# A router's scratch moved from the value products' PSUM bank to banks of its own and to SBUF

## The chip, the cores and the metric

One Trainium2 chip (trn2), one NeuronCore. The metric is the time of one execution on the device in microseconds (us); all times below are in us unless marked otherwise.

## What is computed

Attention over 4 batches, 8 heads, 768 tokens of 64 values, in which a query sees only keys with the same 6-bit hash; then a mixture of experts over the 3072 tokens of 512 values, each going to the one of 8 experts with the largest logit.

```python
q_bucket = sum((q @ proj > 0) * powers); k_bucket = sum((k @ proj > 0) * powers)
scores = where(q_bucket == k_bucket, scale * q @ k.T, -1e9)
x = (softmax(scores) @ v).transpose(0, 2, 1, 3).reshape(B * S, H * D)
logits = x @ w_gate + modality_bias[modality_id]
e_idx = argmax(logits); gate_w = max(softmax(logits))
out[e_idx == e] = gate_w * (relu(x @ w1[e]) @ w2[e])      # for each expert e
```

## The kernel before

`attention()` (L92) runs over 16 pairs of heads, four pairs for a batch. For each pair TensorE computes score tiles, first for the row maxima (`psm`, maxima by VectorE at L241 and L247, two tiles ahead at most) and then for the exponentials (`pss`, L295 and L296, exponentials by ScalarE at L307 and L314 into `pb`); GpSimd adds the `pb` tiles for the row sums (L317, `sp`); TensorE multiplies them with the values (L341, `psu`); ScalarE copies the result to `ut` (L346), which gives the two tiles of `psu` back to the next pair; L359 turns `sp` into sums.

Before a pair's softmax its queries' and keys' hash bits are prepared two pairs ahead (L200, L222). The order of TensorE and of SyncE's queue is written by hand: loop i goes over one pair, and a string of the table PLAN for each of its six rows names what comes next: S two score matmuls' worth, M a maximum, T the preparation, A value products, Q sums, x and y the transposes of `finish_x` (L417, `xs`), G, g, h, k, f, e, w, E one piece of the list of pieces that finishes a batch. VectorE, ScalarE and GpSimd get their order from a scheduler that goes by the order of the program.

When four pairs are done their batch is finished piece by piece: `finish` (L366) sums over the heads into `gl` and the logits (L399 to L403), `route` (L598) takes the maximum (`rm`), the exponent (`rex`), and the one-hot of the chosen expert (`oh`, L612), counts with twelve small matmuls how many tokens chose which expert before each token (L617, L619; the running counts are `run`), forms the gate (L629 to L631) and the token's place in the table (`posi`, L637), and scatters six columns of it with indirect DMAs issued by GpSimd (L642). Batch 0 is finished in the loops of pairs 4 to 7, batch 1 in 8 to 11, batch 2 in 12 to 15, batch 3 in the expert stage. A generator yields once for each piece; in `finish_last` (L426) the first UPTO pieces of batch 2 run, then the early slots (`early_slots`, L708: which blocks of which expert can be gathered before the last batch is routed), then their tables are loaded through SyncE's queue (`early_tables`, L724), then batch 2's scatters.

Router temporaries do not have tiles of their own while attention runs. `Spots` (L80) hands out columns 256 to 512 of `psu1`, the PSUM bank whose first 256 columns are the second part of the value products:

```python
shared = ps_u.tile([P, MAIN], F32, name="psu1")
spot.psum = shared[:, REST:MAIN]
...
t["u"] = [ps_u.tile([P, MAIN], F32, name="psu0"), shared[:, 0:REST]]
```

The waits between engines are kept for a tile, so a row of VectorE in this scratch and a value product of TensorE wait for each other. In the profile both are named `psu`. After attention the scratch is an SBUF tile (`spot.psum = None`, L518).

Of the kernel before, what the change touches and what calls it, by code (L numbers as in the profile page):

```python
# [28 lines left out]
P = 128  # L29
# [4 lines left out]
RELIEF = ()  # L34
UPTO = 12
PLAN = (
# [42 lines left out]

class Spots:  # L80

    psum = None

    def __call__(self, pool, shape, name, at):
        if self.psum is None:
            return pool.tile(shape, F32, name=name)
        n = int(np.prod(shape[1:]))
        ap = self.psum[:, at:at + n]
        return ap if len(shape) == 2 else ap.rearrange("p (a e) -> p a e", a=shape[1])


def attention(ctx, actx, tc, a, x_d, route, setup, early_slots, early_tables, latest, adds, bias, later, spot):  # L92
    nc = tc.nc
# [16 lines left out]
    sm = actx.enter_context(tc.tile_pool(name="sm", bufs=4))  # L110
# [25 lines left out]
    ident = fconst.tile([P, P], F32, name="ident")  # L136
# [192 lines left out]
    def weigh():  # L329

        for i in range(NPR):
            t = st[i]
            t["u"] = [ps_u.tile([P, MAIN], F32, name="psu0"), shared[:, 0:REST]]
            for part in range(2):
                w = COLS[part].stop - COLS[part].start
                nc.tensor.matmul(t["u"][part][:, 0:w], vsb[i % 2], t["lone"][:, COLS[part]], start=True, stop=False, skip_group_check=True)
            for kt in range(NT):
                for part in range(2):
                    w = COLS[part].stop - COLS[part].start
                    for h in range(2):  # L340
                        nc.tensor.matmul(t["u"][part][64 * h:64 * h + 64, 0:w], t["v"][:, h, kt], t["pb"][kt][:, h, COLS[part]], start=False, stop=(kt == NT - 1), skip_group_check=True)  # L341
                if kt == NT - 1:
                    ut = upool.tile([P, S], F32, name="ut")
                    for part in range(2):
                        w = COLS[part].stop - COLS[part].start
                        nc.scalar.copy(out=ut[:, COLS[part]], in_=t["u"][part][:, 0:w])  # L346
                    t["ut"] = ut
                yield
# [17 lines left out]
    def finish(b):  # L366
# [23 lines left out]
        gl = bp.tile([P, NT, 9, 8], F32, name="gl")  # L390
        with tc.issue_after(exps[0]):
            nc.scalar.copy(out=gl[:, :, 8], in_=bias[:, b * NT:(b + 1) * NT])
        for w in range(2):
            n = 4 if w == 0 else 2
# [6 lines left out]
            yield  # L401
        lg = spot(bp, [P, NT, 8], "lg", 0)
        nc.vector.tensor_reduce(out=lg, in_=gl.rearrange("p t h e -> p t e h"), axis=AX.X, op=ALU.add)  # L403
        yield
        yield from route(b, lg, ps_x)

# [42 lines left out]
    with tc.manual_schedule(engines={mybir.EngineType.PE, mybir.EngineType.SP}):  # L449
# [67 lines left out]
        sums(NPR - 1)  # L517
        spot.psum = None  # L518
    return finish, finish_x, ps_x, ident


N = B * S
E = 8
# [6 lines left out]
EARLY = CFG["early"]  # L530
EARLYB = 2
# [17 lines left out]
def router(ctx, tc, a, x_d, tab):  # L549
    nc = tc.nc  # L550
# [44 lines left out]

    scattered, latest, adds, later, counts, spot = [], [], [], [], [], Spots()

    def route(b, lg, ps):  # L598
        l = lg
        m = wk.tile([P, NT], F32, name="rm")  # L600
        nc.vector.tensor_reduce(out=m, in_=l, axis=AX.X, op=ALU.max)
        d = spot(wk, [P, NT, E], "rd", 48)
        nc.vector.tensor_tensor(out=d, in0=l, in1=m.unsqueeze(2).broadcast_to([P, NT, E]), op=ALU.subtract)
        ex = wk.tile([P, NT, E], F32, name="rex")
        nc.scalar.activation(ex, d, AF.Exp)
        yield
        w = spot(wk, [P, NT, E], "rw", 96)
        nc.vector.scalar_tensor_tensor(out=w, in0=d, scalar=0.0, in1=rev.unsqueeze(1).broadcast_to([P, NT, E]), op0=ALU.is_ge, op1=ALU.mult)
# [3 lines left out]
        nc.vector.tensor_tensor(out=oh, in0=w, in1=wm.unsqueeze(2).broadcast_to([P, NT, E]), op=ALU.is_equal)  # L612
        yield
        pp = ps.tile([P, HALF], F32, name="psx")
        for j in range(NT):
            lhs = tri if j == 0 else onesb
            nc.tensor.matmul(pp[:, j * E:NT * E], lhs, oh[:, 0:NT - j].rearrange("p t e -> p (t e)"), start=(j == 0), stop=False, skip_group_check=True)  # L617
        for j in range(NT):
            nc.tensor.matmul(pp[:, 64:64 + E], onesb, oh[:, j], start=False, stop=(j == NT - 1), skip_group_check=True)  # L619
        rk = spot(wk, [P, NT, E], "rk", 144)  # L620
        nc.vector.tensor_tensor(out=rk, in0=pp[:, 0:NT * E].rearrange("p (t e) -> p t e", e=E), in1=run[b % 2].unsqueeze(1).broadcast_to([P, NT, E]), op=ALU.add)
        if b == EARLYB - 1:
            counts.append(spot(wk, [P, E], "counts", 200))
            nc.vector.tensor_tensor(out=counts[0], in0=run[b % 2], in1=pp[:, 64:64 + E], op=ALU.add)
        nc.vector.tensor_tensor(out=run[(b + 1) % 2], in0=run[b % 2], in1=pp[:, 64:64 + E], op=ALU.add)
        yield
        rec = recs[:, b]
        sm = spot(wk, [P, NT], "rsum", 192)
        nc.vector.tensor_reduce(out=sm, in_=ex, axis=AX.X, op=ALU.add)  # L629
        nc.vector.tensor_scalar(out=sm, in0=sm, scalar1=1e-9, scalar2=None, op0=ALU.add)  # L630
        nc.vector.reciprocal(rec[:, :, 1].bitcast(F32), sm)  # L631
        yield
        nc.vector.tensor_tensor(out=rk, in0=rk, in1=oh, op=ALU.mult)
        pos = spot(wk, [P, NT], "pos", 192)
        nc.vector.tensor_reduce(out=pos, in_=rk, axis=AX.X, op=ALU.add)
        posi = wk.tile([P, NT], I32, name="posi", bufs=2)
        nc.vector.tensor_copy(out=posi, in_=pos)  # L637
        yield
# [19 lines left out]
    def above(cnt, row, name):  # L658
        g = spot(wk, [P, E, 12], "sg", 0)
        nc.vector.tensor_tensor(out=g, in0=cnt.unsqueeze(2).broadcast_to([P, E, 12]), in1=step[:, row], op=ALU.is_gt)  # L660
        nb = spot(wk, [P, E], name, 208)
        nc.vector.tensor_reduce(out=nb, in_=g, axis=AX.X, op=ALU.add)
        return nb

    def cumulate(nb, name):
        c2 = spot(wk, [P, E, E], "sc2", 96)
        nc.vector.tensor_tensor(out=c2, in0=low, in1=nb.unsqueeze(1).broadcast_to([P, E, E]), op=ALU.mult)
        cu = spot(wk, [P, E], name, 216)
        nc.vector.tensor_reduce(out=cu, in_=c2, axis=AX.X, op=ALU.add)
        cx = spot(wk, [P, E], name + "x", 224)  # L670
        cs = cu
        if spot.psum is not None:
            cs = wk.tile([P, E], F32, name=name + "s")
            nc.vector.tensor_reduce(out=cs, in_=c2, axis=AX.X, op=ALU.add)
        nc.vector.tensor_tensor(out=cx, in0=cs, in1=nb, op=ALU.subtract)
        return cu, cx

    def assign(n, cu, cx, first, size, out):

        sel = spot(wk, [P, n, E], f"sel{n}", 160)  # L680
        sl = slot[:, 0:n].unsqueeze(2).broadcast_to([P, n, E])
# [4 lines left out]
        nc.vector.tensor_tensor(out=t, in0=sel, in1=eid.unsqueeze(1).broadcast_to([P, n, E]), op=ALU.mult)  # L686
        r = spot(wk, [P, n], f"selr{n}", 192)
        nc.vector.tensor_reduce(out=r, in_=t, axis=AX.X, op=ALU.add)
        nc.vector.tensor_copy(out=out[:, 0], in_=r)
        yield  # L690
        w = spot(wk, [P, E], "selw", 232)
        if size:
# [363 lines left out]
```

## Time and profile before

| | before |
|---|---|
| median of 3 runs | 790.35 us (789.85 to 791.34) |
| the profiled execution, own time | 790.72 us |
| its span | 788.9 us |
| TensorE busy | 747.6 us (95%) |
| VectorE busy | 477.8 us (61%) |
| ScalarE busy | 414.8 us (53%) |
| GpSimd busy | 445.6 us (56%) |

The profile is of one execution. The span goes from the first to the last instruction. An engine's busy time is what its instructions take; time in front of a row in square brackets is idle time of that engine, with the instruction whose end released it. PE is TensorE, DVE VectorE, ACT ScalarE, POOL GpSimd, SP SyncE. A name such as L341 is a line of the kernel.

### The profile page before, as it was taken

Reading aid. Unit: us, or ns where it says so; the run is one execution under the profiler, and the core shown is the slowest. Engines: PE = TensorE matmul, PEld = TensorE weight load, DVE = VectorE, ACT = ScalarE, POOL = GpSimd, SP = SyncE. Lnnn points to the kernel's source line nnn. Section 1 sums busy time; section 2 is a strip of 40 time slices with the busy share of each in tenths; the row PEclk is TensorE's granted clock in tenths of the full one; section 3 lists DMA queues with packets and bytes.
Section 4 is the critical chain, followed back from the end, with each engine's and each line's share of the span. In section 5 each row is a group of like instructions: output and inputs, shape, how many; then the busy total and the mean of one; then the engine's idle time right before and its main releaser. Section 6 shows DMA issues by size and latency. Waiting matters only on the chain.

```text
span 788.9 us, 11622 instructions
## 1 busy us (share of the span) xinstructions
PE 747.6 (95%) x4060; PEld 520.3 (66%) x4060; DVE 477.8 (61%) x829; ACT 414.8 (53%) x732; POOL 445.6 (56%) x325
## 2 busy tenths in 40 slices
PE   5899999999999999999998999999999999999996
PEld 2565566555656566665555546878888888888885
DVE  5777677577777768767766667744344343742422
ACT  3666576666557566666554455333243334643423
POOL 7398988788779888879885982123220204302002
PEclk9999999999999999999999999999999999999999
DMA  6665554264346434454400737376443435844411
GB/s 195 153 189 160 160 130 131 62 160 114 104 126 183 101 97 113 118 170 121 121 22 28 138 77 265 122 126 200 141 139 103 149 105 182 287 117 134 120 55 61
DMA packets 59573, 104.11 MB, mean 132 GB/s; under 512 B 9709, under 2 KB 30957, under 8 KB 59504
## 3 DMA queue, kind: packets, MB, share of 16 engines
q1 hardware_dynamic: 53424, 88.10, 41.0%
q0 software_dynamic: 4928, 13.14, 5.1%
q10 hardware_dynamic: 1152, 2.03, 0.9%
q8 instruction: 34, 0.56, 0.3%
q14 instruction: 35, 0.29, 0.1%
HBM read 59.76 MB, written 13.33 MB: 93 GB/s over the span
## 4 chain that ended last, share of the span: by engine, by line
PE 65%; DVE 11%; issue 10%; ACT 5%; DMA 4%; POOL 3%; SPq 1%; POOLq 0%; ACTq 0%; DVEq 0%
PE psu L341 12%; PE pss L295 8%; PE pss L296 6%; PE hps L846 4%; PE hps L848 4%; PE hps L847 4%; PE yps L892 4%; PE yps L890 4%; PE yps L891 4%; PE psm L239 4%; PE psm L245 2%; ACT pb L307 2%; DVE b_1g L176 2%; PE psx L359 1%; DVE a_0g L266 1%
## 5 line engine op out<-in xcount | busy, mean ns | idle before, releaser
L317 POOL TENSOR_TENSOR sp<-sp,pb 128x768 f32<-128x768 f32 x124 | 233.2, 1908 | 40.5 <-ACT pb L314 37.2
L307 ACT ACTIVATE pb<-pss 128x512 f32<-128x512 f32 x192 | 114.4, 598 | 112.8 <-PE pss L296 96.6
L241 DVE TENSOR_REDUCE mx<-psm 128x1 f32<-128x512 f32 x192 | 130.6, 687 | 55.8 <-PE psm L239 54.8
L341 PE MATMUL psu<-pb,vt 128*64 128x512 f32 (+1 forms) x768 | 136.8, 497 | 4.9 <-DVE eslot L703 2.6
L799 DVE TENSOR_TENSOR w<-raw,w 128x1024 fp32r<-128x1024 f32 x64 | 79.5, 1249 | 94.8 <-ACT w L797 77.2
L797 ACT CAST w<-raw 128x1024 fp32r<-128x1024 f32 x64 | 66.9, 1050 | 73.9 <-PE yps L892 62.7
L341 PEld LDWEIGHTS psu<-pb,vt 128*64 128x64 f32 x768 | 50.9, 138 | 76.2 <-issue 56.4
L817 POOL DMA_INDIRECT xg<-x_d,tb x18 | 22.5, 1248 | 117.8 <-DMA tb<-tab 113.5
L295 PE MATMUL pss<-a_0g 128*128 128x512 f32 x192 | 80.3, 418 | 2.6 <-ACT pb L307 1.7
L890 PE MATMUL yps<-w,hl 128*128 128x512 f32 x208 | 82.7, 398 | 0.0
L892 PE MATMUL yps<-w,hh 128*128 128x512 f32 x208 | 81.3, 391 | 0.0
L891 PE MATMUL yps<-w,hh 128*128 128x512 f32 x208 | 80.9, 389 | 0.0
L846 PE MATMUL hps<-xh,w 128*128 128x512 f32 x192 | 75.6, 394 | 0.8 <-DVE hl L853 0.8
L847 PE MATMUL hps<-xl,w 128*128 128x512 f32 x192 | 74.9, 390 | 0.1
L848 PE MATMUL hps<-xh,w 128*128 128x512 f32 x192 | 74.8, 390 | 0.0
L295 PE MATMUL pss<-a_1g 128*128 128x512 f32 x192 | 67.5, 352 | 4.0 <-ACT pb L314 4.0
L247 DVE TENSOR_REDUCE mx<-psm 128x2 f32<-128x512 f32 x96 | 66.2, 689 | 8.1 <-PE psm L245 4.7
L317 POOL TENSOR_TENSOR sp<-pb,pb 128x768 f32<-128x768 f32 x31 | 56.7, 1850 | 25.2 <-ACT pb L314 25.1
L852 ACT ACTIVATE hh<-hps 128x512 fp32r<-128x512 f32 x48 | 28.6, 598 | 74.5 <-PE hps L848 72.8
L296 PE MATMUL pss<-b_0g 128*128 128x512 f32 x192 | 65.3, 340 | 0.2 <-DMA b_0g<-a_0g 0.2
L296 PE MATMUL pss<-b_1g 128*128 128x512 f32 x192 | 65.0, 339 | 0.0
L853 DVE SCALAR_TENSOR_TENSOR hl<-hps,hh 128x512 fp32r<-128x512 f32 x48 | 33.0, 688 | 52.7 <-ACT hh L852 52.6
(228 smaller groups left out, 1350.2 us busy)
## 6 DMA issues: line engine op xcount, KB each, us to landing
raw<-moe_w SPq DMA_DIRECT2D x64, 512.0 KB
xt<-qk SPq DMA_DIRECT2D x31, 384.0 KB
vt<-v SPq DMA_DIRECT2D x16, 384.0 KB
a_0g<-hx SPq DMA_DIRECT2D x30, 192.0 KB
a_1g<-hx SPq DMA_DIRECT2D x30, 192.0 KB
x_d<-xs SPq DMA_DIRECT2D x18, 256.0 KB
b_1g<-a_1g SPq DMA_DIRECT2D x17, 192.0 KB
b_0g<-a_0g SPq DMA_DIRECT2D x17, 192.0 KB
```

The source lines that it names most:

```text
L241: newest[:] = [nc.vector.tensor_reduce(out=mx[:, qt + j, 1 - h, 0:1], in_=mp, axis=AX.X, op=ALU.max).ins]
L295: nc.tensor.matmul(out, t["s1"][h][:, ks], t["m1"][h][:, cs], start=True, stop=False)
L296: nc.tensor.matmul(out, t["s2"][h][:, ks], t["m2"][h][:, cs], start=False, stop=True)
L307: nc.scalar.activation(t["pb"][kt][:, h, 0:MAIN], sp, AF.Exp, scale=0.125)
L317: add = (nc.vector if h and i in CFG["spd"] else nc.gpsimd).tensor_tensor(out=t["sp"][:, h], in0=(t["pb"][0] if kt == 1 else t["sp"])[:, h ...
L341: nc.tensor.matmul(t["u"][part][64 * h:64 * h + 64, 0:w], t["v"][:, h, kt], t["pb"][kt][:, h, COLS[part]], start=False, stop=(kt == NT - 1 ...
L846: nc.tensor.matmul(hps, lo[:, c, fs], xh[:, c], start=(c == 0), stop=False)
L847: nc.tensor.matmul(hps, hi[:, c, fs], xl[:, c], start=False, stop=False)
L848: nc.tensor.matmul(hps, hi[:, c, fs], xh[:, c], start=False, stop=(c == 3))
L890: nc.tensor.matmul(yps[g], hl[fc][:, gs], hi[:, fb], start=(fc == 0), stop=False)
L891: nc.tensor.matmul(yps[g], hh[fc][:, gs], lo[:, fb], start=False, stop=False)
L892: nc.tensor.matmul(yps[g], hh[fc][:, gs], hi[:, fb], start=False, stop=(fc == 7))
```

## The change

`Spots` is gone. `route` takes `gl`, sums it itself, and is two pieces with PSUM scratch of its own: one tile of the pool `psx` (two banks, also used by transposes, sums and the pattern matmuls) for the logits, their differences and the masked weights, and the rank matmuls' own tile for the ranks, the places and the gate's sum. The value products have `psu0` and `psu1` to themselves. The tables of the early slots (`sg`, `enb`, `sc2`, `ecu`, `ecux`, `sel`, `selr`, `selw`) are SBUF tiles of the pool `wk`. `route` yields twice where it had five yields, and `finish` has one fewer, so UPTO is 8 instead of 12 and every piece behind comes four tokens earlier. The second reduction `ecus`, the copy `counts` and the tile `eleft` are gone.

```diff
-UPTO = 12
+UPTO = 8
...
-    shared = ps_u.tile([P, MAIN], F32, name="psu1")
-    spot.psum = shared[:, REST:MAIN]
...
-            t["u"] = [ps_u.tile([P, MAIN], F32, name="psu0"), shared[:, 0:REST]]
+            t["u"] = [ps_u.tile([P, MAIN], F32, name=f"psu{j}") for j in range(2)]
...
-        lg = spot(bp, [P, NT, 8], "lg", 0)
-        nc.vector.tensor_reduce(out=lg, in_=gl.rearrange("p t h e -> p t e h"), axis=AX.X, op=ALU.add)
-        yield
-        yield from route(b, lg, ps_x)
+        yield from route(b, gl, ps_x)
...
-    def route(b, lg, ps):
-        l = lg
+    def route(b, gl, ps):
+        spot = ps.tile([P, 4, NT, E], F32, name="psx")
+        l, d, w = spot[:, 0], spot[:, 1], spot[:, 2]
+        nc.vector.tensor_reduce(out=l, in_=gl.rearrange("p t h e -> p t e h"), axis=AX.X, op=ALU.add)
         m = wk.tile([P, NT], F32, name="rm")
...
         nc.scalar.activation(ex, d, AF.Exp)
-        yield
-        w = spot(wk, [P, NT, E], "rw", 96)
...
         pp = ps.tile([P, HALF], F32, name="psx")
...
-        rk = spot(wk, [P, NT, E], "rk", 144)
+        rk = pp[:, 128:128 + NT * E].rearrange("p (t e) -> p t e", e=E)
...
-        if b == EARLYB - 1:
-            counts.append(spot(wk, [P, E], "counts", 200))
-            nc.vector.tensor_tensor(out=counts[0], in0=run[b % 2], in1=pp[:, 64:64 + E], op=ALU.add)
         nc.vector.tensor_tensor(out=run[(b + 1) % 2], in0=run[b % 2], in1=pp[:, 64:64 + E], op=ALU.add)
-        yield
...
+        nc.vector.tensor_tensor(out=rk, in0=rk, in1=oh, op=ALU.mult)
+        pos, sm = pp[:, 192:192 + NT], pp[:, 224:224 + NT]
+        nc.vector.tensor_reduce(out=pos, in_=rk, axis=AX.X, op=ALU.add)
+        posi = wk.tile([P, NT], I32, name="posi", bufs=2)
+        nc.vector.tensor_copy(out=posi, in_=pos)
         nc.vector.tensor_reduce(out=sm, in_=ex, axis=AX.X, op=ALU.add)
         nc.vector.tensor_scalar(out=sm, in0=sm, scalar1=1e-9, scalar2=None, op0=ALU.add)
         nc.vector.reciprocal(rec[:, :, 1].bitcast(F32), sm)
-        yield
...
     def above(cnt, row, name):
-        g = spot(wk, [P, E, 12], "sg", 0)
+        g = wk.tile([P, E, 12], F32, name="sg")
...
-        nb = spot(wk, [P, E], name, 208)
+        nb = wk.tile([P, E], F32, name=name)
...
-        if spot.psum is not None:
-            cs = wk.tile([P, E], F32, name=name + "s")
-            nc.vector.tensor_reduce(out=cs, in_=c2, axis=AX.X, op=ALU.add)
-        nc.vector.tensor_tensor(out=cx, in0=cs, in1=nb, op=ALU.subtract)
+        nc.vector.tensor_tensor(out=cx, in0=cu, in1=nb, op=ALU.subtract)
...
-        sel = spot(wk, [P, n, E], f"sel{n}", 160)
+        sel = wk.tile([P, n, E], F32, name=f"sel{n}")
...
-        w = spot(wk, [P, E], "selw", 232)
+        w = wk.tile([P, E], F32, name="selw")
...
-        nb = above(counts[0], 0, "enb")
+        nb = above(run[EARLYB % 2], 0, "enb")
```

The scores' lines L295 and L296 become L281 and L282, the maxima's matmuls L239 and L245 become L225 and L231, L341 becomes L327, L617 and L619 become L599 and L601. Names in the rows that follow: `a_0g` and `b_0g` are operands of the scores, `ident` the transposes' identity, `tri` and `onesb` the rank matmuls' fixed matrices, `klow`, `kslot` and `ke` constants of the tables.

TensorE, first row of the plan in pair 6, where batch 0 is finished. Before:

```order
L245 MATMUL psm<-a_0g_106 128x256 x2
L417 MATMUL psx<-ident,ut 128x128 x4
L295 MATMUL pss<-a_0g_120 128x512
L296 MATMUL pss<-b_0g_122 128x512
L239 MATMUL psm<-a_1g_107 128x512
L295 MATMUL pss<-a_1g_121 128x512
```

With the change:

```order
L231 MATMUL psm<-a_0g_106 128x256 x2
L400 MATMUL psx<-ident,ut 128x128 x4
L599 LDWEIGHTS tri
L599 MATMUL psx<-oh,tri 128x48
L599 LDWEIGHTS onesb
L599 MATMUL psx<-oh,onesb 128x40
```

The twelve rank matmuls (the rows with `oh`, and ten more like them) stand behind the transposes of `xs`; before they stood two plan rows later, behind another group of transposes.

TensorE, second row of the plan in pair 12, where batch 2 is finished. Before:

```order
L296 MATMUL pss<-b_1g_109 128x512
L239 MATMUL psm<-a_1g_114 128x512
L282 MATMUL psx<-va_4113,ones_166 128x128
L295 MATMUL pss<-a_0g_106 128x256
L296 MATMUL pss<-b_0g_108 128x256
L295 MATMUL pss<-a_1g_107 128x256
L296 MATMUL pss<-b_1g_109 128x256
L245 MATMUL psm<-a_1g_114 128x256 x2
```

With the change:

```order
L282 MATMUL pss<-b_1g_109 128x512
L225 MATMUL psm<-a_1g_114 128x512
L268 MATMUL psx<-va_4127,ones_165 128x128
L599 LDWEIGHTS tri
L599 MATMUL psx<-oh,tri 128x48
L599 LDWEIGHTS onesb
```

The rank matmuls stand directly behind the one with `va`; before the value products came first, and the ranks a plan row later.

VectorE in pair 13, the early slots' tables. Before:

```order
L675 TENSOR_TENSOR psu_145<-ecus,psu_145 128x8
L419 TENSOR_TENSOR xs<-psx,rin 128x512
L682 TENSOR_TENSOR psu_145<-psu_145,kslot 128x16
L241 TENSOR_REDUCE mx<-psm 128x1
L684 TENSOR_TENSOR selx_4435<-psu_145,kslot 128x16
L241 TENSOR_REDUCE mx<-psm 128x1
L685 TENSOR_TENSOR psu_145<-psu_145,selx_4435 128x16
L289 TENSOR_TENSOR vs_168<-psx,vs_168 32x64
L686 TENSOR_TENSOR selx_4435<-psu_145,ke_66 128x16
L289 TENSOR_TENSOR vs_168<-psx,vs_168 32x64
L688 TENSOR_REDUCE psu_145<-selx_4435 128x2
L247 TENSOR_REDUCE mx<-psm 128x2
```

With the change:

```order
L646 TENSOR_TENSOR ecux<-ecu,enb 128x8
L233 TENSOR_REDUCE mx<-psm 128x2
L653 TENSOR_TENSOR sel_4360<-ecu,kslot 128x16
L655 TENSOR_TENSOR selx_4362<-ecux,kslot 128x16
L241 TENSOR_REDUCE m_4344<-mx 128x8
L656 TENSOR_TENSOR sel_4360<-sel_4360,selx_4362 128x16
L657 TENSOR_TENSOR selx_4362<-sel_4360,ke_66 128x16
L659 TENSOR_REDUCE selr_4366<-selx_4362 128x2
L660 CAST eslot<-selr_4366 128x2
L227 TENSOR_REDUCE mx<-psm 128x1 x2
L233 TENSOR_REDUCE mx<-psm 128x2
L664 TENSOR_TENSOR selw<-ezero,ecux 128x8
```

The same steps stand earlier among the maxima, and their first operands are no longer in `psu`, so two operands lie in SBUF.

## Rows read from the trace of the kernel before

**Rows 1.** The page, part 1: the span, and each engine's busy time, share and instructions
```profile
span 788.9 us, 11622 instructions
...
PE 747.6 (95%) x4060; PEld 520.3 (66%) x4060; DVE 477.8 (61%) x829; ACT 414.8 (53%) x732; POOL 445.6 (56%) x325
```

**Rows 2.** TensorE's waits: line waited <- for, us in all, times, the longest
```profile
PE psx L264 <- ACT nm L257: 5.2, 4, 1.7
PE pss L295 <- ACT pb L314: 4.0, 11, 0.4
```

**Rows 3.** TensorE's timeline, value products: start us, us, instruction, [idle before <- releaser]
```profile
393.93 1.94 PE L341 MATMUL psu<-pb,vt 128*64 128x256 f32 x12 [1.52 <-ACT rex L605]
...
413.02 1.94 PE L341 MATMUL psu<-pb,vt 128*64 128x256 f32 x12 [0.74 <-DVE psu L662]
...
424.23 3.50 PE L341 MATMUL psu<-pb,vt 128*64 128x256 f32 x12 [2.61 <-DVE eslot L703]
```

**Rows 4.** Windows: stretch, us, then the engines' busy us, granted clock, DMA share, GB/s
```profile
424.00:426.00 2.00, 1.77 (x8) 0.78 (x10) 0.16 (x1) 0.00 (x0) 0.75 (x1) 0.50 0.05 9
```

**Rows 5.** VectorE's timeline, route of batch 0
```profile
190.27 1.02 DVE L403 TENSOR_REDUCE psu<-gl 128x48 f32<-128x432 f32 x1
191.19 1.28 DVE L241 TENSOR_REDUCE mx<-psm 128x1 f32<-128x512 f32 x2
192.47 0.69 DVE L247 TENSOR_REDUCE mx<-psm 128x2 f32<-128x512 f32 x1
193.07 0.68 DVE L419 TENSOR_TENSOR xs<-psx,rin 128x512 f32<-128x512 f32 x1
...
198.53 0.22 DVE L608 SCALAR_TENSOR_TENSOR psu<-psu,ke 128x48 f32<-128x48 f32 x1 [2.12 <-ACT ut L346]
```

**Rows 6.** TensorE's timeline: `xs` transposes, batch 0, and `va` matmuls, batch 2
```profile
192.27 0.60 PE L417 MATMUL psx<-ident,ut 128*128 128x128 f32 x4
...
390.31 0.38 PE L282 MATMUL psx<-va,ones 128*128 128x128 f32 x2
```

**Rows 7.** VectorE's timeline, route of batch 2
```profile
390.48 1.00 DVE L403 TENSOR_REDUCE psu<-gl 128x48 f32<-128x432 f32 x1
391.40 0.67 DVE L241 TENSOR_REDUCE mx<-psm 128x1 f32<-128x512 f32 x1
392.08 0.46 DVE L289 TENSOR_TENSOR vs<-psx,vs 32x64 fp32r<-32x64 f32 x2
...
396.38 0.22 DVE L608 SCALAR_TENSOR_TENSOR psu<-psu,ke 128x48 f32<-128x48 f32 x1 [2.75 <-ACT ut L346]
```

**Rows 8.** TensorE's timeline: waits for `run` and `sp`
```profile
507.67 0.63 PE L417 MATMUL psx<-ident,ut 128*128 128x128 f32 x4 [0.46 <-DVE run L625]
...
452.90 0.84 PE L359 MATMUL psx<-sp,ones 128*32 128x384 f32 x4 [0.67 <-POOL sp L317]
454.65 0.84 PE L359 MATMUL psx<-sp,ones 128*32 128x384 f32 x4 [0.92 <-POOL sp L317]
```

**Rows 9.** VectorE and GpSimd meeting: two-operand rows of both
```profile
242.18 1.04 DVE L176 TENSOR_TENSOR b_1g<-xt,hx 128x768 fp32r<-128x768 f32 x1
...
213.49 2.36 DVE L176 TENSOR_TENSOR b_1g<-xt,hx 128x768 fp32r<-128x768 f32 x1
...
211.41 3.63 POOL L317 TENSOR_TENSOR sp<-sp,pb 128x768 f32<-128x768 f32 x2 [1.78 <-ACT pb L314]
...
450.33 5.10 DVE L317 TENSOR_TENSOR sp<-pb,pb 128x768 f32<-128x768 f32 x1
```

**Rows 10.** VectorE's timeline: a small row of the early tables beside a GpSimd add
```profile
422.57 0.17 DVE L693 TENSOR_TENSOR psu<-ezero,psu 128x8 f32<-128x8 f32 x1
```

**Rows 11.** Windows, line L317 alone: busy us of VectorE and GpSimd, count
```profile
396.00:421.00 25.00, 0.00 (x0) 14.47 (x8) 1.00 0.06 17
```

**Rows 12.** VectorE's timeline: idle ahead of a maximum and of `a_0g`
```profile
410.13 0.69 DVE L241 TENSOR_REDUCE mx<-psm 128x1 f32<-128x512 f32 x1 [0.70 <-PE psm L239]
...
415.30 0.43 DVE L266 SCALAR_TENSOR_TENSOR a_0g<-psx,a_0g 64x256 fp32r<-64x256 f32 x1 [1.02 <-PE psx L264]
```

More of the change, by code (lines that the diff above doesn't have):

```diff
@@ L77, in host_layout, with attention @@
     }
[L80 to L92, printed above, removed]
+def attention(ctx, actx, tc, a, x_d, route, setup, early_slots, early_tables, latest, adds, bias, later):
     nc = tc.nc
@@ L517, in attention @@
         sums(NPR - 1)
-        spot.psum = None
     return finish, finish_x, ps_x, ident
@@ L594, in setup @@
             nc.gpsimd.tensor_copy(out=recs[:, :, :, 0], in_=tok)
-    scattered, latest, adds, later, counts, spot = [], [], [], [], [], Spots()
-    def route(b, lg, ps):
-        l = lg
+    scattered, latest, adds, later = [], [], [], []
+    def route(b, gl, ps):
+        spot = ps.tile([P, 4, NT, E], F32, name="psx")
+        l, d, w = spot[:, 0], spot[:, 1], spot[:, 2]
+        nc.vector.tensor_reduce(out=l, in_=gl.rearrange("p t h e -> p t e h"), axis=AX.X, op=ALU.add)
         m = wk.tile([P, NT], F32, name="rm")
         nc.vector.tensor_reduce(out=m, in_=l, axis=AX.X, op=ALU.max)
-        d = spot(wk, [P, NT, E], "rd", 48)
         nc.vector.tensor_tensor(out=d, in0=l, in1=m.unsqueeze(2).broadcast_to([P, NT, E]), op=ALU.subtract)
@@ L613, in route @@
         yield
+        rec = recs[:, b]
         pp = ps.tile([P, HALF], F32, name="psx")
@@ L619, in route @@
             nc.tensor.matmul(pp[:, 64:64 + E], onesb, oh[:, j], start=False, stop=(j == NT - 1), skip_group_check=True)
-        rk = spot(wk, [P, NT, E], "rk", 144)
+        rk = pp[:, 128:128 + NT * E].rearrange("p (t e) -> p t e", e=E)
         nc.vector.tensor_tensor(out=rk, in0=pp[:, 0:NT * E].rearrange("p (t e) -> p t e", e=E), in1=run[b % 2].unsqueeze(1).broadcast_to([P, NT, E]), op=ALU.add)
-        if b == EARLYB - 1:
-            counts.append(spot(wk, [P, E], "counts", 200))
-            nc.vector.tensor_tensor(out=counts[0], in0=run[b % 2], in1=pp[:, 64:64 + E], op=ALU.add)
         nc.vector.tensor_tensor(out=run[(b + 1) % 2], in0=run[b % 2], in1=pp[:, 64:64 + E], op=ALU.add)
-        yield
-        rec = recs[:, b]
-        sm = spot(wk, [P, NT], "rsum", 192)
+        nc.vector.tensor_tensor(out=rk, in0=rk, in1=oh, op=ALU.mult)
[3 more added lines that the diff above has]
+        nc.vector.tensor_copy(out=posi, in_=pos)
         nc.vector.tensor_reduce(out=sm, in_=ex, axis=AX.X, op=ALU.add)
@@ L631, in route @@
         nc.vector.reciprocal(rec[:, :, 1].bitcast(F32), sm)
-        yield
[L633 to L637, printed above, removed]
         yield
@@ L665, in cumulate @@
     def cumulate(nb, name):
-        c2 = spot(wk, [P, E, E], "sc2", 96)
+        c2 = wk.tile([P, E, E], F32, name="sc2")
         nc.vector.tensor_tensor(out=c2, in0=low, in1=nb.unsqueeze(1).broadcast_to([P, E, E]), op=ALU.mult)
-        cu = spot(wk, [P, E], name, 216)
+        cu = wk.tile([P, E], F32, name=name)
         nc.vector.tensor_reduce(out=cu, in_=c2, axis=AX.X, op=ALU.add)
-        cx = spot(wk, [P, E], name + "x", 224)
-        cs = cu
-        if spot.psum is not None:
-            cs = wk.tile([P, E], F32, name=name + "s")
-            nc.vector.tensor_reduce(out=cs, in_=c2, axis=AX.X, op=ALU.add)
-        nc.vector.tensor_tensor(out=cx, in0=cs, in1=nb, op=ALU.subtract)
+        cx = wk.tile([P, E], F32, name=name + "x")
+        nc.vector.tensor_tensor(out=cx, in0=cu, in1=nb, op=ALU.subtract)
         return cu, cx
     def assign(n, cu, cx, first, size, out):
-        sel = spot(wk, [P, n, E], f"sel{n}", 160)
+        sel = wk.tile([P, n, E], F32, name=f"sel{n}")
         sl = slot[:, 0:n].unsqueeze(2).broadcast_to([P, n, E])
@@ L686, in assign @@
         nc.vector.tensor_tensor(out=t, in0=sel, in1=eid.unsqueeze(1).broadcast_to([P, n, E]), op=ALU.mult)
-        r = spot(wk, [P, n], f"selr{n}", 192)
+        r = wk.tile([P, n], F32, name=f"selr{n}")
         nc.vector.tensor_reduce(out=r, in_=t, axis=AX.X, op=ALU.add)
@@ L715, in early_slots @@
         yield from assign(EARLY, cu, cx, zero, TS, eslot)
-        left = wk.tile([P, E], F32, name="eleft")
-        nc.vector.tensor_scalar(out=left, in0=cx, scalar1=-1.0, scalar2=float(EARLY), op0=ALU.mult, op1=ALU.add)
-        nc.vector.scalar_tensor_tensor(out=early, in0=left, scalar=0.0, in1=nb, op0=ALU.max, op1=ALU.min)
+        nc.vector.tensor_scalar(out=early, in0=cx, scalar1=-1.0, scalar2=float(EARLY), op0=ALU.mult, op1=ALU.add)
+        nc.vector.scalar_tensor_tensor(out=early, in0=early, scalar=0.0, in1=nb, op0=ALU.max, op1=ALU.min)
         yield
@@ L755, in late_slots @@
         return big, sml, tot
-    return route, early_slots, early_tables, (eslot, etb, ete), late_slots, setup, latest, adds, bias, later, spot
+    return route, early_slots, early_tables, (eslot, etb, ete), late_slots, setup, latest, adds, bias, later
 def experts(ctx, tc, a, x_d, tab, out, ps_x, ident, first, adds):
@@ L1012, in body @@
     with ExitStack() as ctx, ExitStack() as actx:
-        route, early_slots, early_tables, early_tiles, late_slots, setup, latest, adds, bias, later, spot = router(ctx, tc, a, x_d, tab)
-        finish, finish_x, ps_x, ident = attention(ctx, actx, tc, a, x_d, route, setup, early_slots, early_tables, latest, adds, bias, later, spot)
+        route, early_slots, early_tables, early_tiles, late_slots, setup, latest, adds, bias, later = router(ctx, tc, a, x_d, tab)
+        finish, finish_x, ps_x, ident = attention(ctx, actx, tc, a, x_d, route, setup, early_slots, early_tables, latest, adds, bias, later)
         actx.close()
```

## The prediction

> **What bounds the kernel now.** I read the page's first part, then TensorE's waits, then the timelines of TensorE, VectorE and GpSimd around the router. TensorE is busy for 747.6 of 788.9 us, VectorE, ScalarE and GpSimd for 61% or less [rows 1], so what counts is whether TensorE's few idle stretches go or new ones come. The list of its waits holds the preparation's wait for `nm`, 5.2 in four, and the scores' for `pb`, 4.0 in eleven [rows 2], and three of the value products for rows of the bank the change takes apart. The timeline shows these in their places, all in the route of batch 2 and the early tables: 1.52 ahead of 393.93 (for `rex`), 0.74 ahead of 413.02 (a table), 2.61 ahead of 424.23 (`eslot`) [rows 3]. The reader sees one thing more there: twelve value products took 1.94 after the first two stalls and 3.50 after the third. The windows show why: the granted clock is 0.50 in 424 to 426 [rows 4], that is 1.2 GHz instead of 2.4 after 2.61 us of idling. That stall so cost 2.61 + (3.50 - 1.94) = 4.17.
>
> **What the change removes.** The value products no longer share a bank with router work, so the three stalls go: 1.52 + 0.74 + 2.61, and 1.56 of half clock, 6.43 in all. VectorE's own waits for the `ut` copy, 2.75 ahead of `w` in batch 2 [rows 7], go too; they cost TensorE nothing by themselves, since the rank matmuls ran much later. In the expert stage the transposes of batch 3 waited 0.46 for `run` [rows 8]; the ranks now come several matmul groups earlier: 0.46. The scatters of batch 2 on GpSimd come four pieces earlier, and the adds of the last pair with them; `L359` waited 0.67 and 0.92 for those adds [rows 8]. Nothing in before shows how much of this goes; it lies between 0 and 1.59, and I take the longer one, 0.92, since each is shorter than one add (3.63 / 2 [rows 9]) and several scatters leave that stretch. Sum of gains: 6.43 + 0.46 + 0.92 = 7.81. Four small VectorE rows fewer change nothing: VectorE is not the bound.
>
> **What it adds: ranks too close behind the one-hot.** With one piece per chain, the twelve rank matmuls stand two PLAN rows earlier, as the order shows. In batch 0 (and batch 1, whose rows read alike) they come directly behind the `xs` transposes, which end at 192.27 + 0.60 = 192.87 [rows 6]. Their operand `oh` comes out of VectorE's queue: the sum over heads ends at 190.27 + 1.02 = 191.29, and behind it stand three maxima (1.28 + 0.69), one `xs` (0.68) and five small ones (`rm`, `d`, `w`, `rwm`, `oh`, some 0.2 each as `w` shows) [rows 5]. Laid end to end that is 194.94, a stall of 2.07; independent rows follow each other about 0.1 before the last one ends (191.19 against 191.29), and with that for all eight steps it is 1.3. I take 1.6, twice: 3.2. No other matmul can slip by: TensorE's order is written by hand, and the score matmuls behind it wait too.
>
> In batch 2 the ranks come directly behind the `va` matmuls, free at 390.31 + 0.38 = 390.69 [rows 6]. The reduction ends at 390.48 + 1.00 = 391.48; then a maximum (0.67), two `vs` (0.46) and the five small ones [rows 7] give 393.6: a stall of 2.9. So the 1.52 that goes is replaced by a longer wait some matmuls earlier. An idle stretch of 2.61 was followed by the half clock in before; one of 1.52 was not [rows 3, 4]. 2.9 lies above both, so I add the same 1.56 again. Ends: 2.4 without a drop, 4.5 with.
>
> **What it adds: tables in SBUF.** The early slots' tables were in PSUM; now twelve VectorE rows of some 0.2 us read two SBUF operands (`sg`, `sc2`, `ecux`, four for the first selection, `selw` twice, `selx` twice, `early`). They stand in VectorE's queue between the maxima, of which TensorE can be only two tiles ahead, so a late maximum stops it. No row of before is such a small instruction beside a GpSimd add. The nearest are large: `b_1g`, two SBUF operands, takes 1.04, but 2.36 at 213.49, where it meets an add begun at 211.41; and one of VectorE's own adds takes 5.10 at 450.33 while two GpSimd adds run [rows 9]. An operation on one PSUM operand takes 0.17 in the middle of an add [rows 10]. So the lower end is 0 (small rows slip through, as with PSUM) and the upper one is twelve whole adds of 3.63 / 2 = 1.82: 21.8. Between them: adds cover 14.47 of the 25 us from 396 to 421 [rows 11], 58%; a row that starts at random waits half an add, 0.91, so 12 x 0.58 x 0.91 = 6.3. VectorE's idle time in this stretch takes some of it: 0.70 and 1.02 [rows 12]. I take 6.3 - 1.7 = 4.6.
>
> The Trainium skill, "SBUF — State Buffer", section "SBUF: two separate sides", speaks against this part: a VectorE instruction with two SBUF inputs and a GpSimd one that reads SBUF hold the port pair they share exclusively, for the whole instruction, whoever came first. The trace agrees for large rows (2.36 and 5.10 above). By that rule the size of the VectorE instruction would not matter: each of the twelve would wait for the rest of an add, and the sum would hold the 6.3 instead of the 4.6, that is 796.5 instead of 794.8.
>
> **Small parts.** Slot loads now stand ahead of the last `vt` load on SyncE's queue; the values of the last pair are needed a pair later, so 0. The exp of the router on ScalarE reads a PSUM tile of its own instead of the shared one and stands between the same exponentials: 0.
>
> **Sum.** 3.2 + 2.9 + 1.56 + 4.6 - 7.81 = +4.45. The profiled execution took 790.72 (span 788.9), 0.37 above the median of 790.35; put on the median: **794.8**.
>
> **Rivals.**
> *Small rows slip through.* PSUM-operand rows of 0.17 never grew beside an add, and if small SBUF rows behave so, the 4.6 is nothing: 4.45 - 4.6 = -0.15, so 790.2, no measurable change (0.2% is 1.6 us, about what a measurement of this kernel can tell). Against it: `b_1g`.
> *Faster.* The same, and the stalls at the ranks are also returned: in the pairs with batches 0 and 1 TensorE waits for ScalarE anyway (`nm` 5.2 over four times, `pb` 4.0 over eleven [rows 2]), and if it arrives 1.6 later those are over. Then 3.2 goes, and if the clock holds through batch 2's stall 1.56 as well: 790.35 - 0.15 - 3.2 - 1.56 = 785.4; with half of that, 787.8. Decides: whether the adds, maxima and exps run ahead while TensorE waits. For it: VectorE and ScalarE have a third of their time free. Against: the waits for `nm` hang on the maxima, which are behind the same queue.
> *Much slower.* Each small row, released by one add, meets the next, because GpSimd starts it first (450.33 was passed over once [rows 9]). Then 21.8 instead of 4.6: 790.35 + 4.45 + 17.2 = 812.0; half of them, 10.9: 801.1, and one more drop of the clock 802.7.
> *It doesn't do what it says.* TensorE's value products would still wait for router rows; the order has none in that bank, so this has 2 in 100, at 790.
>
> **How the numbers follow.** Forecast 0.42, small rows slip through 0.16, faster 0.25, much slower 0.15, nothing 0.02. The range reaches to 785.4 and 803 and leaves out what lies beyond, above all the heavier half of the slowest case. The likeliest case by itself runs from 789.8 (stalls of 1.3 twice and 2.4 and half the port term: 2.6 + 2.4 + 2.3 - 7.81 = -0.5) to 797.5 (2.07 twice, 4.5 and 6.3: 14.94 - 7.81 = +7.1). Faster than 0.2%: 0.27 (the faster case and a bit of the next). Within 0.2%: 0.16. Slower: 0.57.
>
> **What would show it.** Right: in the profile after, no wait of L327 (the value products) for anything of VectorE; a wait of L599 for `oh` of some 1.6 twice and 2.9 once, the last with half clock behind it; VectorE rows L635 to L688 of 1 to 2 us instead of 0.2 where a GpSimd add runs, and waits of the maxp matmuls for `mx` between 395 and 425. Wrong: L635 to L688 all at 0.2; L599 waiting less than 1 us, or total TensorE idle time no larger than now.

## The result and the profile after

The change is slower: 794.8 us median of 11 runs (792.35 to 796.66) against 790.35 of 11 runs of the kernel before on the same chips, a ratio of 1.0064 with a 95% interval of 1.0044 to 1.0084. The forecast was 794.8, slower, with a range of 785.4 to 803. The sum came out; the sections below show that several of its terms did not.

The page after, part 1, to set against [rows 1]:

```profile
span 792.1 us, 11620 instructions
...
PE 749.5 (95%) x4060; PEld 523.5 (66%) x4060; DVE 484.3 (61%) x827; ACT 415.4 (52%) x732; POOL 446.5 (56%) x325
```

VectorE is busy for 6.5 us more although it runs two rows fewer (827 against 829); something on it takes longer. TensorE's waits after, to set against [rows 2]:

```profile
PE psx L250 <- ACT nm L243: 7.2, 3, 3.9
PE psx L599 <- DVE oh L593: 6.2, 3, 3.0
...
PE psm L231 <- DVE mx L227: 2.2, 4, 1.2
```

No wait of the value products (L327) is left: the three of [rows 3] are gone. In their place stand 6.2 us for `oh`, and one wait of 3.9 for `nm`, the row maxima on their way into the scores. TensorE's timeline shows where:

```profile
194.41 0.20 PE L599 MATMUL psx<-oh,tri 128*128 128x48 bf16 x1 [1.56 <-DVE oh L593]
...
308.35 0.20 PE L599 MATMUL psx<-oh,tri 128*128 128x48 bf16 x1 [1.55 <-DVE oh L593]
...
395.50 0.18 PE L599 MATMUL psx<-oh,tri 128*128 128x48 bf16 x1 [3.04 <-DVE oh L593]
...
396.85 4.27 PE L327 MATMUL psu<-pb,vt 128*64 128x512 f32 x16
...
408.13 0.51 PE L231 MATMUL psm<-a_1g 128*128 128x256 f32 x2 [1.24 <-DVE mx L227]
...
408.91 2.80 PE L327 MATMUL psu<-pb,vt 128*64 128x512 f32 x16
...
424.94 0.50 PE L250 MATMUL psx<-identr,nm 128*128 128x128 f32 x2 [3.91 <-ACT nm L243]
...
425.79 0.63 PE L282 MATMUL pss<-b_0g 128*128 128x512 f32 x1
```

The rank matmuls wait in all three batches. Behind the 3.04 sixteen value products take 4.27; the same sixteen take 2.80 at 408.91, where the granted clock is 1.00. Behind the 3.91 a score matmul takes 0.63 instead of 0.39. The windows (stretch, us, the engines' busy us, granted clock, DMA share, GB/s) give the clock behind each gap:

```profile
194.40:196.40 2.00, 2.00 (x17) 1.68 (x18) 0.90 (x4) 0.80 (x2) 0.00 (x0) 0.66 0.78 220
196.40:198.40 2.00, 2.00 (x9) 1.82 (x8) 1.41 (x5) 1.01 (x3) 0.46 (x1) 0.50 0.35 108
...
308.30:310.00 1.70, 1.65 (x18) 1.44 (x19) 0.95 (x4) 0.78 (x2) 0.00 (x0) 1.00 0.70 216
...
397.50:399.50 2.00, 2.00 (x10) 0.75 (x8) 2.00 (x6) 0.00 (x0) 2.00 (x2) 0.50 0.02 4
...
426.00:428.00 2.00, 2.00 (x6) 1.50 (x6) 1.94 (x6) 1.44 (x3) 0.00 (x0) 0.50 0.04 2
```

0.50 is 1.2 GHz. The clock fell behind the gap of 1.56, the one of 3.04 and the one of 3.91, and not behind the one of 1.55. VectorE's timeline in the early slots' tables, and GpSimd's in the same stretch:

```profile
405.58 1.89 DVE L642 TENSOR_TENSOR sc<-klow,enb 128x64 f32<-128x64 f32 x1
...
409.71 1.25 DVE L653 TENSOR_TENSOR sel<-ecu,kslot 128x16 f32<-128x16 f32 x1
410.89 1.87 DVE L655 TENSOR_TENSOR selx<-ecux,kslot 128x16 f32<-128x16 f32 x1
...
413.00 0.18 DVE L657 TENSOR_TENSOR selx<-sel,ke 128x16 f32<-128x16 f32 x1
413.21 0.17 DVE L659 TENSOR_REDUCE selr<-selx 128x2 f32<-128x16 f32 x1
...
416.36 1.77 DVE L667 SCALAR_TENSOR_TENSOR selw<-selw,ke 128x8 f32<-128x8 f32 x1
418.05 0.68 DVE L227 TENSOR_REDUCE mx<-psm 128x1 f32<-128x512 f32 x1
418.65 1.26 DVE L668 TENSOR_SCALAR selw<-selw 128x8 f32<-128x8 f32 x1
419.95 1.74 DVE L670 SCALAR_TENSOR_TENSOR selx<-kslot,selw 128x16 f32<-128x16 f32 x1
```

```profile
405.55 7.18 POOL L303 TENSOR_TENSOR sp<-sp,pb 128x768 f32<-128x768 f32 x4 [3.45 <-ACT pb L300]
416.23 7.18 POOL L303 TENSOR_TENSOR sp<-sp,pb 128x768 f32<-128x768 f32 x4 [3.50 <-ACT pb L300]
```

Eight elements take 1.77 us while adds run (416.23 to 423.41), and sixteen take 0.18 while none does (413.00). Nine of the 21 table rows are long; above 0.17 each they lose 11.5 us. Maxima stand between them in VectorE's queue; the last of these maxima come late, and so do `m` and `nm`, which are made from them. For that `nm` TensorE waits 3.91.

The account, from the start of the same instruction in both profiles:

| start of | before | after | shift | gained or lost since the row above |
|---|---|---|---|---|
| hash matmuls (L200, now L186), pair ahead of batch 0's route | 170.64 | 170.60 | -0.04 | |
| the same, pair ahead of batch 1's | 283.16 | 284.84 | +1.68 | +1.72 batch 0 |
| the same, pair after batch 1's | 366.56 | 368.30 | +1.74 | +0.06 batch 1 |
| the same, pair of batch 2's ranks | 396.47 | 401.71 | +5.24 | +3.50 batch 2's ranks |
| sums (L359, now L345) behind the tables | 427.65 | 435.61 | +7.96 | +2.72 tables |
| first matmul into `psu` of the last pair (L336, now L322) | 460.27 | 465.60 | +5.33 | -2.63 sums of `sp` |
| end of span | 788.9 | 792.1 | +3.2 | -2.1 expert stage |

The twelve rank matmuls of batch 2, 0.3 us of work, stand ahead of the fourth row's hash matmuls with the change and behind them before; so 0.3 of its +3.50 belongs to the row below.

### The profile page after: what moved, and what is told of

Same layout as the page of the kernel before. It is cut to its first block, busy times and chain, and to the rows that moved or that the text cites. A ratio compares the mean times of both kernels' runs of the same rounds, so it can differ in the third digit from the quotient of the medians.

```text
span 792.1 us, 11620 instructions
## 1 busy us (share of the span) xinstructions
PE 749.5 (95%) x4060; PEld 523.5 (66%) x4060; DVE 484.3 (61%) x827; ACT 415.4 (52%) x732; POOL 446.5 (56%) x325
## 4 chain that ended last, share of the span: by engine, by line
PE 67%; DVE 12%; issue 10%; ACT 5%; DMA 3%; POOL 2%; SPq 1%; POOLq 0%; ACTq 0%; DVEq 0%
PE psu L327 12%; PE pss L281 8%; PE pss L282 6%; PE hps L816 4%; PE hps L818 4%; PE hps L817 4%; PE psm L225 4%; PE yps L862 4%; PE yps L860 4%; PE yps L861 4%; PE psm L231 2%; ACT pb L293 2%; DVE mx L227 2%; DVE a_0g L252 2%; DVE mx L233 2%
## 5 line engine op out<-in xcount | busy, mean ns | idle before, releaser
L327 PE MATMUL psu<-pb,vt 128*64 128x512 f32 (+1 forms) x768 | 135.9, 496 | 0.0
L327 PEld LDWEIGHTS psu<-pb,vt 128*64 128x64 f32 x768 | 51.3, 138 | 70.2 <-issue 60.2
L281 PE MATMUL pss<-a_0g 128*128 128x512 f32 x192 | 80.6, 420 | 3.1 <-ACT pb L293 2.1
L281 PE MATMUL pss<-a_1g 128*128 128x512 f32 x192 | 68.2, 355 | 3.8 <-ACT pb L300 3.8
L282 PE MATMUL pss<-b_0g 128*128 128x512 f32 x192 | 65.9, 343 | 0.0
L282 PE MATMUL pss<-b_1g 128*128 128x512 f32 x192 | 65.6, 342 | 0.0
```

The source lines that it names most:

```text
L281: nc.tensor.matmul(out, t["s1"][h][:, ks], t["m1"][h][:, cs], start=True, stop=False)
L282: nc.tensor.matmul(out, t["s2"][h][:, ks], t["m2"][h][:, cs], start=False, stop=True)
```

## Experiments

Ratios are to the kernel before, which ran beside each; the change has 1.0064.

**Ranks two pieces later.** The gap ahead of the ranks taken away.

```diff
-UPTO = 8
+UPTO = 10
...
         nc.vector.tensor_tensor(out=oh, in0=w, in1=wm.unsqueeze(2).broadcast_to([P, NT, E]), op=ALU.is_equal)
         yield
+        if b < B - 1:
+            yield
+            yield
```

> The change with the rank matmuls of batches 0 to 2 put back two plan rows later (two empty pieces behind the one-hot, so what follows, tables and scatters, comes two pieces later too). Theory A (ranks too close behind the one-hot): the three waits for oh (1.56, 1.55, 3.04) shrink below 0.3 each and the half clock behind the first and the third goes; the waits for nm in the pairs behind batches 0 and 1 come back with about 1 us each; 5 to 7 us less than the change, 788 to 790. Rival B (TensorE was going to wait there for ScalarE and GpSimd anyway): the waits turn up later under another name, less than 2 us gained, 793 to 795.

Measured: 792.34, ratio 1.0029 (1.0011 to 1.0047). The waits for `oh` are gone; the gain of 2.5 us in the medians lies between the two theories, and the two intervals still touch (1.0047 against 1.0044). TensorE's waits say why it is no more:

```profile
PE psx L345 <- POOL sp L303: 3.1, 2, 2.2
PE psx L250 <- DVE recs L615: 2.1, 2, 1.1
...
PE psx L250 <- ACT a_0g L210: 1.2, 2, 0.6
```

The sums wait for adds again (tables and scatters had moved two pieces, too), and behind that the clock fell to half, as the window shows:

```profile
456.00:458.00 2.00, 2.00 (x7) 0.76 (x8) 0.55 (x1) 0.00 (x0) 1.96 (x2) 0.50 0.18 29
```

The maxima's transposes wait for `recs`, the end of the gate, which holds the rank matmuls' tile, one of two banks of `psx`. In this run the table rows lose only 4.0 us instead of 11.5, though they are in SBUF as in the change: the place counts. So A holds for the waits at the ranks, not for the time: part of the gain was spent on new waits.

**Scatters four pieces later.**

```diff
         puts = [partial(put, t) for t in range(NT)]
...
+        if b == EARLYB:
+            for _ in range(4):
+                yield
         for p in puts:
```

> The change with four empty pieces ahead of batch 2's scatters, so that these come in the places they had before; all else stays. Theory A (the 2.5 us that the change wins back around the last pair's sums come from the earlier scatters): the waits of the sums' matmuls for sp return, 1.6 to 2.5 us in all, 796.5 to 797.5. Rival B (TensorE comes later there, so GpSimd has caught up whatever the scatters do): no such wait, within 0.7 us of the change, 794 to 795.5.

Measured: 797.42, ratio 1.0078 (1.0055 to 1.0102). The waits of the sums are back, in its timeline:

```profile
461.89 0.84 PE L345 MATMUL psx<-sp,ones 128*32 128x384 f32 x4 [0.86 <-POOL sp L303]
463.65 0.84 PE L345 MATMUL psx<-sp,ones 128*32 128x384 f32 x4 [0.92 <-POOL sp L303]
```

That answers to the 0.67 and 0.92 of [rows 8], so the earlier scatters are what took them away. The time agrees with A; its interval overlaps that of the change, so the 2.6 us between the medians are not shown by the time alone.

**Tables back in the shared bank**, route as in the change. The cut is against the kernel before.

```diff
-UPTO = 12
+UPTO = 8
...
-    def route(b, lg, ps):
+    def route(b, gl, ps):
+        spot = ps.tile([P, 4, NT, E], F32, name="psx")
...
     def above(cnt, row, name):
         g = spot(wk, [P, E, 12], "sg", 0)
```

(`above`, `cumulate` and `assign` are those of the kernel before; `route` is that of the change.)

> The change with the early slots' tables back in columns 256 to 512 of the value products' bank, route as in the change. Theory A (table rows in SBUF wait for the GpSimd adds and so delay maxima): the table rows take 0.2 again, the waits of 1.24 for mx and 3.91 for nm go, waits of the value products for a table or eslot return, up to 3.4 us, perhaps with half clock; 2 to 4 us less than the change, 791 to 793. Rival B (those waits come from the ranks' delay, not from the tables): the wait for nm stays over 2 us and the time is that of the change or more, 795 to 798.

Measured: 791.36, ratio 1.0017 (1.0001 to 1.0032). No wait for `nm` at that place; the wait for `eslot` is back and slows the products behind it:

```profile
411.24 0.18 DVE L678 TENSOR_TENSOR selx<-psu,kslot 128x16 f32<-128x16 f32 x1
...
418.25 0.17 DVE L693 SCALAR_TENSOR_TENSOR selx<-kslot,psu 128x16 f32<-128x16 f32 x1
```

```profile
420.23 3.38 PE L341 MATMUL psu<-pb,vt 128*64 128x256 f32 x12 [2.36 <-DVE eslot L697]
```

The ranks' delay is the same as in the change (3.04 ahead of 395.41), and the wait of 3.91 is not there: it came from the tables in SBUF. A holds, and the interval lies clear of that of the change.

**Tables alone in SBUF**, all else as before, except that the copy `counts`, the second reduction `ecus` and the tile `eleft` are gone as in the change. The cut is against the kernel before.

```diff
-        g = spot(wk, [P, E, 12], "sg", 0)
+        g = wk.tile([P, E, 12], F32, name="sg")
...
-        c2 = spot(wk, [P, E, E], "sc2", 96)
+        c2 = wk.tile([P, E, E], F32, name="sc2")
...
-        sel = spot(wk, [P, n, E], f"sel{n}", 160)
+        sel = wk.tile([P, n, E], F32, name=f"sel{n}")
```

> The kernel before with the early slots' tables alone moved to SBUF; route, its scratch and its pieces as before. Theory A: VectorE's two-operand table rows take 1.2 to 1.9 where a GpSimd add runs, TensorE loses the waits of 0.7 and 2.6 and the half clock (4.9) and gains waits for mx and nm of 5 to 8: 790.5 to 794. Rival B (the tables' rows find room between the maxima): only the 4.9 are lost: 785 to 787.

Measured: 787.75, ratio 0.9965 (0.9950 to 0.9981): faster than before. Rows of VectorE and TensorE:

```profile
418.26 2.25 DVE L664 TENSOR_TENSOR sc<-klow,enb 128x64 f32<-128x64 f32 x1
...
423.37 0.15 DVE L689 SCALAR_TENSOR_TENSOR selw<-selw,ke 128x8 f32<-128x8 f32 x1
```

```profile
421.18 0.50 PE L245 MATMUL psm<-a_0g 128*128 128x256 f32 x2 [1.98 <-DVE mx L241]
```

Here most table rows fall between 421.8 and 426.4, where no add runs, and take 0.15 to 0.18; four are long and lose 4.8 us, of which TensorE sees 1.98 and a half clock behind it:

```profile
423.00:425.00 2.00, 2.00 (x9) 1.71 (x8) 1.94 (x8) 1.11 (x4) 0.18 (x1) 0.50 0.00 0
```

The time is nearer to B, but the mechanism of A is there in the long rows. Both expectations took the price of the tables as fixed; this run and the next show that it hangs on their place.

**Tables four pieces later**, and batch 2's scatters behind them, ranks as in the change.

```diff
-UPTO = 8
+UPTO = 12
...
         nc.vector.reciprocal(rec[:, :, 1].bitcast(F32), sm)
         yield
+        if b == EARLYB:
+            for _ in range(4):
+                yield
```

> The change with four empty pieces ahead of the early slots' tables alone: ranks stay close behind the one-hot, tables and scatters come where they came before. Theory A (what the SBUF tables cost hangs on where in the pair they stand among the maxima and the GpSimd adds): the rows' waiting falls from 11 us to about 4 as in the run with SBUF tables alone, the wait of 3.91 for nm falls below 1.5, the waits of the sums for sp (1.6) come back: 789.5 to 792. Rival B (the delay comes from the ranks of batch 2, whatever the tables' place): the wait for nm stays near 3.9 and the time is 795 to 797.

Measured: 791.7, ratio 1.0005 (0.9987 to 1.0023). The ranks wait 3.04 as in the change; the table rows lose 6.0 us instead of 11.5, and of TensorE's waits behind them this is the longest:

```profile
423.28 0.50 PE L231 MATMUL psm<-a_0g 128*128 128x256 f32 x2 [1.24 <-DVE mx L227]
```

The wait of 3.91 is gone, and of the sums' waits for `sp` only one of 0.92 came back. A holds: with the same rows in SBUF moved by four pieces the median is some 3 us lower than the change's, and the intervals of the two do not overlap. The scatters that moved with them are no rival: late by themselves, they did not make the change faster (797.42 above).

**Everything in its old place, scratch as in the change.** Two empty pieces ahead of the ranks, two ahead of the tables.

```diff
-UPTO = 8
+UPTO = 12
...
         yield
+        if b < B - 1:
+            yield
+            yield
...
         yield
+        if b == EARLYB:
+            for _ in range(2):
+                yield
```

> The change with ranks two pieces later and tables and scatters four pieces later, so that all stand where they stood before, with only the scratch moved: route in banks of its own, tables in SBUF. Theory A: no wait for oh over 0.3, none of the value products for router rows, tables' rows waiting some 4 us in all; against the kernel before with SBUF tables only the wait of 1.52 for rex is gone: 785.5 to 787.5. Rival B (route's scratch in the psx banks costs something by itself, as the two waits of 1 us for recs in the run with late ranks hint): 788.5 to 791.

Measured: 787.74, ratio 0.9951 (0.9932 to 0.9971): faster than the kernel before. Expected by A was up to 787.5; the waits named by B are there (`recs` 2.2 in two), so both are in part right. Between this run and the one before it the place of the tables and of batch 2's scatters is the same, and only the ranks, with the scatters of batches 0 and 1 behind them, moved by two pieces: 787.74 against 791.7, with intervals that do not overlap. This is where the price of the early ranks shows in the time. Three rows of its timelines, two of VectorE and one of GpSimd, show that a table row with a single SBUF operand can wait for an add, too:

```profile
425.70 1.57 DVE L666 CAST eslot<-selr 128x2 int32<-128x2 f32 x1
427.18 1.93 DVE L676 SCALAR_TENSOR_TENSOR selx<-kslot,selw 128x16 f32<-128x16 f32 x1
```

```profile
425.38 3.69 POOL L303 TENSOR_TENSOR sp<-pb,pb 128x768 f32<-128x768 f32 x2 [0.20 <-ACT pb L300]
```

The CAST ends with the first of the two adds (425.38 + 1.85), and the row behind it with the second.

**Scatters two to a piece**, on top of that.

```diff
-        for p in puts:
+        for n, p in enumerate(puts):
             p()
-            if b < B - 1:
+            if b < B - 1 and n % 2:
                 yield
```

> The same with batch 2's six scatters issued two to a piece, so that they end three pieces earlier. Theory A (the sums of the last pairs wait for adds that stand behind scatters): the waits for sp of 1.6 or more go, 1 to 2.5 us less than the run before it in this list. Rival B (two scatters in a row hold up the adds of the pair ahead): the same wait at another sum, no gain.

Measured: 788.89, ratio 0.9973 (0.9956 to 0.9990). The wait for `sp` is gone, and this one stands in its place:

```profile
448.45 0.39 PE L281 MATMUL pss<-a_0g 128*128 128x256 f32 x1 [2.41 <-ACT pb L293]
```

Behind it the clock fell to half:

```profile
450.50:452.50 2.00, 2.00 (x9) 1.81 (x8) 0.00 (x0) 1.40 (x3) 2.00 (x2) 0.50 1.32 81
```

No gain, as B expected, though the wait has another name than B's; that the paired scatters cause it was not shown.

**The gate in a tile of its own**, on top of everything in its old place.

```diff
         yield
         rec = recs[:, b]
+        if b < B - 1:
+            yield
+        sm = ps.tile([P, NT], F32, name="psx")
+        nc.vector.tensor_reduce(out=sm, in_=ex, axis=AX.X, op=ALU.add)
+        nc.vector.tensor_scalar(out=sm, in0=sm, scalar1=1e-9, scalar2=None, op0=ALU.add)
+        nc.vector.reciprocal(rec[:, :, 1].bitcast(F32), sm)
+        if b < B - 1:
+            yield
         pp = ps.tile([P, HALF], F32, name="psx")
```

(The same three rows behind the ranks are taken out; the two yields shown take the place of the two empty pieces.)

> The run with everything in its old place, and the gate's sum and reciprocal taken out of the rank matmuls' tile into a small tile and piece of their own ahead of the ranks. Theory A (in that run the row-maximum transposes wait 1.1 twice for recs, because the rank tile is held until the gate is done, one of two psx banks): both waits shrink by 0.5 or more, 0.8 to 1.5 us less than that run, ratio to before 0.992 to 0.9945. Rival B (the transposes wait there for nm from ScalarE anyway): the waits carry another name and the ratio stays at 0.995.

Measured: 786.0, ratio 0.9943 (0.9923 to 0.9963). No wait for `recs` is left, and no other took its place; that much of A is shown. The step from 0.9951 to 0.9943 lies within the intervals. This is the fastest kernel of the study by its median, and faster than both kernels beyond its interval.

## Why the prediction was right, point by point

The five terms, in the profiled execution, against the account above: they add up to +4.45 in the prediction and to +3.2 in the two profiles; the medians differ by 4.45. That the median was met to the last digit is luck: the terms erred by some 3 us at most, in both directions.

*What the change removes.* The three waits of the value products and the half clock behind the third are gone, as forecast. The two waits of 0.67 and 0.92 for `sp` both went, not one, and with them TensorE lost less around them: -2.63 instead of -0.92. In the expert stage the wait of 0.46 for `run` went, and two more that the prediction did not have, 0.63 for `hl` and 0.55 for `xl`; of the -2.1 these three explain 1.64, the rest was not traced. Only the 0.46 goes with the new route: in the run with the tables alone in SBUF, whose route is that of before, it is still there, but the 0.55 is gone and the 0.63 is down to 0.17.

*Ranks behind the one-hot, batches 0 and 1.* 1.56 and 1.55 where 1.6 was forecast: the sum over VectorE's rows was right. But the term as a whole, +3.2, measured +1.8. In batch 0 the half clock came behind the wait, which I had not expected at 1.56 since the gap of 1.52 in [rows 3] had none; with waits alike in both batches, their rows in the account differ by 1.72 - 0.06 = 1.66, about what the half clock costs. Against it, the pair behind each rank lost a wait of TensorE for `nm` and smaller ones. In before:

```profile
217.88 0.37 PE L264 MATMUL psx<-identr,nm 128*128 128x128 f32 x2 [1.15 <-ACT nm L257]
...
330.14 0.37 PE L264 MATMUL psx<-identr,nm 128*128 128x128 f32 x2 [0.94 <-ACT nm L257]
```

That give-back was a rival's, "Faster", and it happened in these two batches; the part of that rival in which tables cost nothing did not.

*Batch 2.* 3.04 for 2.9, and the half clock behind it (4.27 - 2.80 = 1.47 on the value products), as forecast: +3.50, or 3.2 without the rank matmuls themselves, against 2.9 + 1.56 - 1.52 = 2.94.

*Tables in SBUF.* The mechanism is right: rows of some 0.2 us grew to 1.2 to 1.9 beside an add, and each of the eight rows with two SBUF operands that met an add waited for its end, so that small rows did not slip through. The size is the term that was mis-sized: rows and waits cost TensorE some 2.72 + 0.3 + 4.91 (the removed 0.74, 2.61 and 1.56) = 7.9 where 4.6 stood. The two waits that came of them, 1.24 + 3.91 = 5.15, are near the 4.6, but only because two errors offset each other: the rows lost 11.5 us instead of 6.3, and of that not 1.7 but more than 6 never became such a wait of TensorE. What the term lacked was above all the half clock behind the 3.91, a cost the forecast had in its "Much slower" rival alone. The matmuls from 425.24 to 430.26 took 5.02:

```profile
425.24 0.76 PE L281 MATMUL pss<-a_0g 128*128 128x512 f32 x1
...
430.26 0.62 PE L281 MATMUL pss<-a_0g 128*128 128x512 f32 x1
```

The same matmuls took 2.92 in before, where the granted clock is 1.00:

```profile
415.10 0.46 PE L295 MATMUL pss<-a_0g 128*128 128x512 f32 x1
...
418.02 0.50 PE L295 MATMUL pss<-a_0g 128*128 128x512 f32 x1
```

That is 2.10. With 1.66 and 1.47 above, the half clock behind these three gaps took some 5.2 us in the change, against 1.56 in the kernel before; the difference, 3.7, is more than the 3.2 between the two profiles.

In the 11.5 two steps failed. I had each long row wait half an add on average; a row that is let in between two adds is followed by one that meets the next add from its start, as L653 and L655 (1.25, then 1.87) and L668 and L670 (1.26, then 1.74) do. And I counted only rows with two SBUF operands. L668, a TENSOR_SCALAR with one, took 1.26, and in the run with everything in its old place a CAST with one took 1.57, while the reductions on one SBUF operand took 0.25 or less beside adds. The Trainium skill, "SBUF — State Buffer", section "Who interferes with whom", names casts and `tensor_scalar` among the instructions that can take the shared ports; these two rows agree with it, and I had used only the rule on two inputs.

*What I did not see at all* is that the price of the tables is not theirs but their place's: 11.5 us of waiting rows at the change's place, 4 to 6 at the others. The SBUF tables alone made the kernel before faster (0.9965), the new route alone made it 1.0017, and both together 1.0064: the pieces that the new route saves move the tables to where the adds run.

Three places are named wrongly ahead of the prediction, and one count in it; no term of the sum hangs on them. In batch 0 the ranks moved by two pieces, and these are four plan rows there, not two. The place shown for batch 2 is in the loop of pair 13, not 12. The table rows shown of the kernel before are in pair 14; only those of the change are in pair 13. And VectorE has two rows fewer, not four.

## What to carry to other kernels

A list of pieces is also a timetable: whoever merges pieces moves everything behind them, and here the moves cost more (1.0064 against 0.9951) than the new scratch won. Put empty pieces where steps were saved first, and then move one step at a time. Small VectorE rows in SBUF beside GpSimd adds are not small; here either one operand in PSUM or a place between the adds kept them at 0.2 us. And look at the granted clock behind every new gap: here it took some 5.2 us besides the waits themselves.

## What was not expected of the hardware

Gaps of the same length did not act alike on TensorE's clock. In four kernels with the ranks close behind the one-hot, the waits of 1.55 and 1.56 in batches 0 and 1 were followed by the half clock in one of the two batches each: in batch 0 in the change and in the run with tables four pieces later, in batch 1 in the run with tables in the shared bank and in that with late scatters. Each kernel was profiled in one execution, so this need not belong to the kernel. Windows of the last two, behind their gaps, which end at 306.70 and 308.33:

```profile
308.00:310.00 2.00, 2.00 (x8) 1.63 (x6) 0.94 (x3) 1.09 (x2) 0.00 (x0) 0.50 0.68 177
```

```profile
310.00:312.00 2.00, 2.00 (x8) 1.71 (x7) 1.33 (x3) 1.12 (x3) 0.00 (x0) 0.50 0.52 140
```

So a wait of some 1.55 us cost TensorE either that or, with the 1.66 above, some 3.2; which of the two it will be was not settled here.
